# Query projections moved from the MLP blocks to the heads of the layers, and stored in the slots of their transposed input

## The chip, the cores and the metric

One Trainium2 chip, one of its cores. The time is the device time of one execution in microseconds (us). A kernel is run several times, alternating with the kernel before on the same chip; I quote medians with the lowest and highest run. Ratios are the mean time of one kernel's fast runs over the mean time of the other's fast runs of the same rounds, so they are not quite the ratio of the medians that stand beside them. All runs here were of the fast state.

The engines: PE multiplies matrices (PEld is its weight load, which runs beside it: 1082.6 us of PE and 837.1 us of PEld in a span of 1149.5 us), DVE is the vector engine, ACT the scalar engine, POOL is GpSimd, SP starts transfers. The order of each engine's instructions is fixed by the program. In one run below PE idles for 2.09 us in front of a product that waits for DVE, and the ten projection matmuls that are next in its order start only behind it. A wait for a PSUM bank holds PE in the same way: 0.73 us, twice, in the second head of the changed kernel, and the twenty projection matmuls next in its order start behind it.

## The reference, cut to what matters

Two identical layers over 2048 tokens of width 576. Each has a linear attention with 32 heads of 18 channels, whose feature map is a softmax of the projection and one of its negative, and then a gated MLP of width 4608. The weights `w_phi` are folded into the query and key weights at the start of the kernel.

```python
phi_q = concat([softmax(pq), softmax(-pq)])     # pq = x @ Wq @ w_phi, per head of 18
phi_k = concat([softmax(pk), softmax(-pk)])
kv  = einsum("bhsf,bhsd->bhfd", phi_k, v)       # needs every token
num = einsum("bhqf,bhfd->bhqd", phi_q, kv)
o   = num / den                                 # then @ wo, and added to x
...
x = x + A(layernorm(x)); x = x + B(layernorm(x))    # B: (x@Wg * x@Wu) @ Wd
x = x + A(layernorm(x)); x = x + B(layernorm(x))
```

## The kernel before

The 2048 tokens are 16 tiles of 128. A layer begins with a head: keys and values are projected, and the key-value sum is formed, which must be complete before any token's numerator. After it come eight blocks of the MLP, of two tiles each. Within a block PE first does the gate and up matmuls in two halves of its rows at once, then the down matmuls. Queries and the output projection of the tiles of the next block are woven into the gate and up stage, their numerators (products with the key-value sum, which lies in `BD`) into the down matmuls. The keys and values of layer 2 are woven into the blocks of layer 1, up to the last two tiles, which can only be done after its last block: that is the second head.

A query projection inside a block runs in row halves too (18 matmuls of 64 rows), outside it in full height (10 matmuls of 128 rows). Its softmax starts from PSUM, and the two banks are held until DVE has subtracted the minimum:

```python
def softmax_front(self, st_, pz, Wm, km, crit, ev=None, rowonly=False):
    ...
    gots = yield ("acqn", ["pb"], 2, True)              # two PSUM banks
    yield from s.proj(st_, Wm, km, banks)               # PE
    # ACT copies both halves to psb in SBUF; DVE: maximum from psb,
    # two minima from PSUM; POOL subtracts the maximum
    ...
    for h in range(2):
        ops.append(Op(370, (lambda e, ...: e.tensor_tensor(d2h, pv, mnbh, ALU.subtract)), ...))   # DVE, from PSUM
    yield ("ops", "dve", ops)
    for bank in banks:
        yield ("rel", "pb", bank)
    # two exponentials on ACT, their sums on DVE, reciprocals on ACT, two multiplies on POOL
```

A static scheduler, part of the program that builds the kernel, decides the order of each engine's instructions and which of the free PSUM banks each takes. The layer input, normalized and transposed, lies in `xT`, laid out `[128, 5, 2048]`; it is read by the projections and then by gate and up.

## Time and profile before

| | before |
|---|---|
| time, median of 3 | 1154.15 us (1151.78 to 1157.53) |
| span of the profiled run, granted clock | 1149.5 us, 0.983 |
| PE busy | 1082.6 us, 94% |
| DVE, ACT, POOL busy | 54%, 33%, 24% |
| first gate/up of layer 1 | 121.1 us |
| blocks of layer 1, start to start (1 to 5) | 65.3 to 66.0 us |
| block 7 of layer 1 with the second head | 96.5 us |
| blocks of layer 2 (1 to 5) | 59.8 us |

The stages are read from the first gate/up matmul of each block. The page's slices of 1/40 of the span show where PE is not full: the first five slices, and the 23rd and 24th; in the 23rd the clock is lower too. Digits are tenths.

```profile
PE   5776899999999999999999589999999999999998
...
PEclk9899999999999999999999799999999999999999
```

One more view matters later. It is the timeline of PE and DVE around one stall inside a block of layer 2; the columns are start, duration, engine, line, instruction, and in brackets the idle time before it and what ended it.

```profile
884.64 1.35 DVE L968 TENSOR_REDUCE ss<-dd 128x64 f32<-128x1152 bf16 x1 [1.32 <-ACT dd L963]
...
885.91 1.28 DVE L1283 TENSOR_TENSOR hT<-ps,hT 128x512 bf16<-128x512 f32 x2
...
886.65 0.28 PE L1235 MATMUL ps<-xT,Wu 64*128 64x256 bf16 x1 [0.38 <-DVE hT L1283]
```

DVE is far from full, but the sum of a query softmax (1.35 us) stands in its queue ahead of the multiplies of the MLP that empty PE's banks, and PE stands idle for 0.38 us. (From start to start it loses more: the gate/up matmul before this one began at 886.00, and pairs begin 0.11 us apart otherwise, so 0.54 us are lost.)

### The profile page before, as it was taken

Reading aid. Unit: us, or ns where it says so; the run is one execution under the profiler, and the core shown is the slowest. Engines: PE = TensorE matmul, PEld = TensorE weight load, DVE = VectorE, ACT = ScalarE, POOL = GpSimd, SP = SyncE. Lnnn points to the kernel's source line nnn. Section 1 sums busy time; section 2 is a strip of 40 time slices with the busy share of each in tenths; the row PEclk is TensorE's granted clock in tenths of the full one; section 3 lists DMA queues with packets and bytes.
Section 4 is the critical chain, followed back from the end, with each engine's and each line's share of the span. In section 5 each row is a group of like instructions: output and inputs, shape, how many; then the busy total and the mean of one; then the engine's idle time right before and its main releaser. Section 6 shows DMA issues by size and latency. Waiting matters only on the chain.

```text
span 1149.5 us, 34128 instructions
## 1 busy us (share of the span) xinstructions
PE 1082.6 (94%) x15480; PEld 837.1 (73%) x15480; DVE 618.8 (54%) x1289; ACT 376.9 (33%) x860; POOL 281.1 (24%) x304
## 2 busy tenths in 40 slices
PE   5776899999999999999999589999999999999998
PEld 3555777869687786869687368686868686868685
DVE  7788665747465573746352666362636262624131
ACT  7675331504143250514231233140414041312120
POOL 5775230413133240403220222130303030200000
PEclk9899999999999999999999799999999999999999
DMA  8383137282533627271523211827171626353514
GB/s 184 85 297 141 28 79 171 35 208 35 166 67 96 138 34 198 35 197 27 156 64 117 70 22 26 228 34 208 35 200 37 187 50 175 68 149 83 156 43 135
DMA packets 181035, 128.25 MB, mean 112 GB/s; under 512 B 99354, under 2 KB 179738, under 8 KB 179738
## 3 DMA queue, kind: packets, MB, share of 16 engines
q1 hardware_dynamic: 180890, 126.07, 42.7%
q8 instruction: 121, 1.98, 0.7%
q14 instruction: 24, 0.20, 0.1%
HBM read 100.73 MB, written 2.36 MB: 90 GB/s over the span
## 4 chain that ended last, share of the span: by engine, by line
PE 83%; DVE 9%; ACT 4%; DMA 3%; POOL 1%; issue 1%; SPq 0%; DVEq 0%; ACTq 0%
PE ps L1235 44%; PE ps L1305 20%; PE ps L901 9%; PE ps L1308 3%; PE ps L889 2%; PE ps L1134 2%; DVE ss L968 2%; DMA wdr<-in_B_w_down_dram 2%; PE ps L1020 1%; DVE x_sb L1182 1%; POOL dd L979 1%; DVE mxmn L928 1%; DVE mxmn L933 1%; DVE hT L1283 1%; DVE dd L947 1%
## 5 line engine op out<-in xcount | busy, mean ns | idle before, releaser
L1235 PE MATMUL ps<-xT,Wu 64*128 64x256 bf16 x4608 | 589.6, 270 | 2.3 <-DVE hT L1283 1.9
L1235 PE MATMUL ps<-xT,Wg 64*128 64x256 bf16 x4608 | 588.2, 270 | 1.6 <-ACT xT L870 1.6
L1235 PEld LDWEIGHTS ps<-xT,Wu 64*128 64x128 bf16 x4608 | 432.0, 94 | 25.1 <-DVE hT L1283 5.3
L1235 PEld LDWEIGHTS ps<-xT,Wg 64*128 64x128 bf16 x4608 | 427.1, 94 | 29.1 <-issue 3.3
L1281 ACT CAST hT<-ps 128x512 bf16<-128x512 f32 x288 | 167.8, 583 | 558.9 <-PE ps L1235 519.6
L1283 DVE TENSOR_TENSOR hT<-ps,hT 128x512 bf16<-128x512 f32 x288 | 197.5, 689 | 200.7 <-ACT hT L1281 200.3
L1305 PE MATMUL ps<-wdr,hT 128*128 128x512 bf16 x960 | 247.2, 380 | 1.5 <-DMA wdr<-in_B_w_down_dram 1.3
L1235 PE MATMUL ps<-xT,Wr 64*128 64x256 bf16 x1152 | 199.0, 270 | 0.0
L1308 PE MATMUL ps<-wdr,hT 128*128 128x64 bf16 x960 | 185.0, 193 | 0.0
L979 POOL TENSOR_TENSOR dd<-dd,ss 128x576 bf16<-128x576 bf16 x124 | 143.7, 1180 | 148.7 <-ACT ss L975 144.9
L1305 PEld LDWEIGHTS ps<-wdr,hT 128*128 128x128 bf16 x960 | 93.8, 98 | 112.2 <-DMA wdr<-in_B_w_down_dram 4.5
L859 POOL TENSOR_SCALAR xln<-x_sb,nmean,rstd 128x576 bf16<-128x576 bf16 x104 | 62.6, 607 | 413.8 <-ACT rstd L848 358.7
L1330 DVE TENSOR_TENSOR x_sb<-ps,x_sb 128x512 bf16<-128x512 f32 x32 | 22.0, 686 | 205.1 <-PE ps L1308 205.1
L938 POOL TENSOR_TENSOR dd<-psb,mxmn 128x576 bf16<-128x576 bf16 x63 | 73.3, 1164 | 209.1 <-DVE mxmn L928 209.0
L968 DVE TENSOR_REDUCE ss<-dd 128x64 f32<-128x1152 bf16 x64 | 86.3, 1348 | 32.0 <-ACT dd L963 31.4
L1308 PEld LDWEIGHTS ps<-wdr,hT 128*128 128x128 bf16 x960 | 94.1, 98 | 0.0
L1235 PEld LDWEIGHTS ps<-xT,Wr 64*128 64x128 bf16 x1152 | 89.5, 94 | 5.2
L961 ACT ACTIVATE dd<-dd 128x576 bf16<-128x576 bf16 x64 | 43.6, 683 | 54.7 <-DVE dd L947 54.7
L925 ACT CAST psb<-ps 128x288 bf16<-128x288 f32 x128 | 47.4, 400 | 37.5 <-PE ps L901 20.5
L928 DVE TENSOR_REDUCE mxmn<-psb 128x32 f32<-128x576 bf16 x64 | 47.5, 743 | 21.7 <-ACT psb L925 21.4
L1305 PE MATMUL ps<-wdx,hT 128*128 128x512 bf16 x192 | 53.5, 380 | 0.0
L933 DVE TENSOR_REDUCE mxmn<-ps 128x16 f32<-128x288 f32 x128 | 52.0, 448 | 0.0
(87 smaller groups left out, 937.5 us busy)
## 6 DMA issues: line engine op xcount, KB each, us to landing
wdr<-in_B_w_down_dram SPq DMA_DIRECT2D x240, 288.0 KB, 3.8
wdx<-in_B_w_down_dram SPq DMA_DIRECT2D x48, 288.0 KB, 3.7
Wg<-in_B_w_gate_dram SPq DMA_DIRECT2D x4, 1152.0 KB, 12.5
Wu<-in_B_w_up_dram SPq DMA_DIRECT2D x4, 1152.0 KB, 15.2
x_sb<-in_A_x_dram SPq DMA_DIRECT2D x8, 288.0 KB, 3.2
out_dram<-x_sb SPq DMA_DIRECT2D x16, 144.0 KB, 2.4
Wraw<-in_A_wqkv_dram SPq DMA_DIRECT2D x8, 144.0 KB, 3.4
xT<-xln SPq DMA_TRANSPOSE x58, 2.6
```

The lines of the kernel that those rows point to most:

```text
L859: em = [(lambda e, j=j, a=a, b=b, c=c: e.tensor_scalar(xln[:, sl[j], a:b], x_sb[:, ss[j], c:c + b - a], s.nmean[:, sl[j]:sl[j] + 1], rstd[ ...
L901: out.append(Op(61, (lambda e, h=h, k=k, st=(i == 0 and k == 0), sp=(i == 1 and k == 3): e.matmul(s.ps[:, banks[h], 0:N], L[r, k, :], Wm[r ...
L928: ops = [Op(665, (lambda e: e.tensor_reduce(mxmn[:, pz, 0, :], p3, AX.X, ALU.max)), reads=[("psb", pz, 0), ("psb", pz, 1)], writes=[("mx", ...
L933: ops.append(Op(370, (lambda e, h=h, pv=pv: e.tensor_reduce(mxmn[:, pz, 1, 16 * h:16 * h + 16], pv, AX.X, ALU.min)), reads=[("pbd", bank)] ...
L938: yield ("alt", [(eng, [Op(dur, (lambda e: e.tensor_tensor(d1, p3, mxb, ALU.subtract)), reads=[("psb", pz, 0), ("psb", pz, 1), ("mx", pz)] ...
L968: Op(1320, (lambda e: e.tensor_reduce(ss[:, sm, :].rearrange("p (b g) -> p b g", b=2), e4, AX.X, ALU.add)), reads=s.ddk(sm, 0) + s.ddk(sm, ...
L979: yield ("alt", [(eng, [Op(dur, (lambda e, ev=ev, rb=rb: e.tensor_tensor(ev, ev, rb, ALU.mult)), reads=s.ddk(sm, br) + [("ss", sm)], write ...
L1235: out.append(Op(54.3, (lambda e, bank=bank, cs=cs, lhsT=lhsT, rhs=rhs, st=st, sp=sp: e.matmul(ps[:, bank, cs], lhsT, rhs, start=st, stop=s ...
L1281: yield ("ops", "act", [Op(540, (lambda e, gb=gb, p=p: e.copy(hT[:, p, :], ps[:, gb, :])), reads=[("gu", gb)], writes=[("hT", p)] + (s.raw ...
L1283: yield ("ops", "dve", [Op(625, (lambda e, ub=ub, p=p: e.tensor_tensor(hT[:, p, :], ps[:, ub, :], hT[:, p, :], ALU.mult)), reads=[("gu", u ...
L1305: ops.append(Op(d_pe(512), (lambda e, lhsT=lhsT, bank=bank, slot=slot, fi=fi, f=f: e.matmul(ps[:, bank, 0:512], lhsT, s.wslot(slot)[:, fi, ...
L1308: ops.append(Op(d_pe(64) + 3, (lambda e, lhsT=lhsT, sl=sl, slot=slot, fi=fi, f=f: e.matmul(ps[:, Z, 64 * sl:64 * sl + 64], lhsT, s.wslot(s ...
```

## The change

The intent: PE is idle for a third of the heads and hardly at all in the blocks. The change therefore projects fourteen of sixteen query tiles of each layer in the heads, in full height, and parks the result (576 channels) in the slot of the `xT` tile it came from, which is 640 wide; nothing else needs that tile's input any more. The softmax is done later from SBUF, so that it holds no PSUM bank; minimum and maximum are two reductions on DVE, and both subtractions go to POOL. For the slot to be contiguous the layout of `xT` becomes `[128, 16, 5, 128]`, and gate and up read two runs of 128 columns in place of one of 256.

```diff
-        self.xT = A("xT", [128, 5, S], BF16)
+        self.xT = A("xT", [128, NS, 5, 128], BF16)
...
+    def t_qproj(self, L, st_):
+        yield ("wait", ("w", "q"))
+        yield ("wait", ("kp", L, st_))          # key and value of the tile are done
+        yield ("wait", ("v", L, st_))
+        if L == 1:
+            yield ("wait", ("ain", 1, min(NS - 1, s.pqg + st_ // s.pqd)))
+        ...
+        yield from s.proj(st_, s.Wq, "Wq", banks)
+        for h in range(2):                      # ACT: PSUM -> the tile's slot in xT
+            yield ("ops", "act", [... e.copy(s.pq(st_)[:, 288 * h:288 * h + 288], s.ps[:, bank, 0:288]) ...])
+            yield ("rel", "pb", bank)
+
+    def stored_front(self, L, st_):
+        yield ("wait", ("pq", L, st_))
+        for br, alu in ((0, ALU.max), (1, ALU.min)):
+            yield ("ops", "dve", [... e.tensor_reduce(s.mxq[:, mq, br, :], p3, AX.X, alu) ...])
+        for br in range(2):
+            yield ("ops", "pool", [... e.tensor_tensor(d, p3, mb, ALU.subtract) ...])
+        yield from s.softmax_tail(sm, 0)
...
-            ps_ = yield ("acq", "psb")
-            sm = yield from s.softmax_front(st_, ps_, s.Wq, "Wq", ...)
+            if st_ >= 2: sm = yield from s.stored_front(L, st_)
...
-                    seq = [(W[r, k, fs], s.xT[r, k, tok]) for k in range(4)]
+                    seq = [(W[r, k, fs], s.xT[r, tok, k, :]) for k in range(4)]
...
+    def t_qps(self):
+        yield ("wait", ("dn", 1, NB - 1))
+        for st_ in range(2, NS):
+            yield ("go", s.t_qproj(2, st_), s.pqp[1] + (NS - st_) / 100.0, ...)
```

More of the change, by code (lines that the diff above doesn't have):

```diff
@@ L546, in __init__ @@
         self.urgent = 4
+        self.pqp = (5, 5)
+        self.pqg = 12
+        self.pqd = 100
+        self.pqn = (16, 16)
         self.qcrit = False
@@ L600, in alloc @@
         self.dd = A("dd", [128, self.NSM, 2, D], BF16)
+        self.mxq = A("mxq", [128, 2, 2, H], F32)
         self.ss = A("ss", [128, self.NSM, 2 * H], F32)
@@ L613, in alloc @@
         sc.pool("vx", self.NVX)
+        sc.pool("mq", 2)
         sc.pool("et", self.NET)
@@ L863, in t_ln @@
         for j in js:
-            tok = slice(128 * ss[j], 128 * ss[j] + 128)
             if fast:
@@ L869, in t_ln @@
                                         reads=[("xln", sl[j]), ("ident",)], writes=[("pbd", bank)], excl=[("pb", bank)]) for k in range(5)])
-                yield ("ops", "act", [Op(d_act(640, True), (lambda e, P=P, tok=tok: e.copy(xT[:, :, tok], P[:, 0:640].rearrange("p (k n) -> p k n", k=5))),
+                yield ("ops", "act", [Op(d_act(640, True), (lambda e, P=P, j=j: e.copy(xT[:, ss[j], :, :], P[:, 0:640].rearrange("p (k n) -> p k n", k=5))),
                                          reads=[("pbd", bank)], writes=[("xT", ss[j])], excl=[("pb", bank)])])
@@ L873, in t_ln @@
             else:
-                yield ("dma", s.g_xt[sl[j]], (lambda e, j=j, tok=tok: e.dma_start_transpose(xT[:, :, tok], xln[:, sl[j], :])),
+                yield ("dma", s.g_xt[sl[j]], (lambda e, j=j: e.dma_start_transpose(xT[:, ss[j], :, :], xln[:, sl[j], :])),
                        [("xln", sl[j])], [("xT", ss[j])], 128 * 640 * 2, False, True, 1250.0)
@@ L884, in proj @@
         s = self
-        tok = slice(128 * st_, 128 * st_ + 128)
-        L = s.xT[:, :, tok] if src is None else src
+        L = s.xT[:, st_, :, :] if src is None else src
         rd = (keys or [("xT", st_)]) + [(km,), (km, 0)]
@@ L912, in proj, with softmax_front @@
         yield ("boost", 0.0)
-    def softmax_front(self, st_, pz, Wm, km, crit, ev=None, rowonly=False):
+    def softmax_front(self, st_, pz, Wm, km, crit, ev=None, rowonly=False, pev=None):
         s = self
@@ L922, in softmax_front @@
         yield from s.proj(st_, Wm, km, banks)
+        yield ("sig", pev)
         for h in range(2):
@@ L958, in softmax_front, with pq, softmax_tail @@
         yield ("sig", ev)
+        yield from s.softmax_tail(sm, crit, pz)
+        return sm
+    def pq(self, st_):
+        return self.xT[:, st_, :, :].rearrange("p k n -> p (k n)")[:, 0:D]
+    def t_qproj(self, L, st_):
+        s = self
+        yield ("wait", ("w", "q"))
[3 more added lines that the diff above has]
+            yield ("wait", ("ain", 1, min(NS - 1, s.pqg + st_ // s.pqd)))
+        if st_ >= s.pqn[L - 1]:
+            yield ("when", lambda: s.sc.open)
+        gots = yield ("acqn", ["pb"], 2, True)
+        banks = [g_[1] for g_ in gots]
+        yield from s.proj(st_, s.Wq, "Wq", banks)
+        for h in range(2):
+            bank = banks[h]
+            yield ("ops", "act", [Op(d_actc(288), (lambda e, h=h, bank=bank: e.copy(s.pq(st_)[:, 288 * h:288 * h + 288], s.ps[:, bank, 0:288])),
+                                     reads=[("pbd", bank)], writes=[("xT", st_)], excl=[("pb", bank)])])
+            yield ("rel", "pb", bank)
+        yield ("sig", ("pq", L, st_))
+    def stored_front(self, L, st_):
+        s = self
+        yield ("wait", ("pq", L, st_))
+        sm = yield ("acq", "sm")
+        mq = yield ("acq", "mq")
+        p3 = s.pq(st_).rearrange("p (g e) -> p g e", e=DH)
+        for br, alu in ((0, ALU.max), (1, ALU.min)):
+            yield ("ops", "dve", [Op(720, (lambda e, br=br, alu=alu: e.tensor_reduce(s.mxq[:, mq, br, :], p3, AX.X, alu)), reads=[("xT", st_)], writes=[("mq", mq, br)])])
+        for br in range(2):
+            d = s.dd[:, sm, br, :].rearrange("p (g e) -> p g e", e=DH)
+            mb = s.mxq[:, mq, br, :].unsqueeze(2).to_broadcast([128, H, DH])
+            yield ("ops", "pool", [Op(1150, (lambda e, d=d, mb=mb: e.tensor_tensor(d, p3, mb, ALU.subtract)), reads=[("xT", st_), ("mq", mq, br)], writes=s.ddk(sm, br))])
+        yield ("rel", "mq", mq)
+        yield from s.softmax_tail(sm, 0)
+        return sm
+    def softmax_tail(self, sm, crit, pz=None):
+        s = self
+        dd, ss = s.dd, s.ss
         de1 = dd[:, sm, 0, :]
@@ L964, in softmax_front @@
                                  reads=[("dd", sm, 0)], writes=[("dd", sm, 0)])])
-        yield ("rel", "psb", pz)
+        if pz is not None:
+            yield ("rel", "psb", pz)
         e4 = dd[:, sm, :, :].rearrange("p b (g e) -> p b g e", e=DH)
@@ L981, in softmax_front @@
                            for eng, dur in (("pool", 1150), ("dve", 675))[:1 + (crit > 1)]])
-        return sm
     def t_v(self, L, st_):
@@ L1030, in t_ain @@
         yield ("go", s.t_v(L, st_), (11 if L == 2 and st_ >= NS - 2 else 6) + (NS - st_) / 100.0, "v%d_%d" % (L, st_))
-        sm = yield from s.softmax_front(st_, ps_, s.Wk, "Wk", 2 if st_ >= NS - 2 else 1 if L == 1 else 0, None, L == 2 and st_ < NS - 2)
+        sm = yield from s.softmax_front(st_, ps_, s.Wk, "Wk", 2 if st_ >= NS - 2 else 1 if L == 1 else 0, None, L == 2 and st_ < NS - 2, ("kp", L, st_))
         yield ("wait", ("v", L, st_))
@@ L1094, in t_aout @@
         yield ("wait", ("ld", "wo"))
-        ps_ = yield ("acq", "psb")
-        sm = yield from s.softmax_front(st_, ps_, s.Wq, "Wq", 2 if L == 1 and st_ < 2 and s.qcrit else 0, ("qp", L, st_), st_ >= s.urgent)
+        if st_ >= 2:
+            sm = yield from s.stored_front(L, st_)
+        else:
+            ps_ = yield ("acq", "psb")
+            sm = yield from s.softmax_front(st_, ps_, s.Wq, "Wq", 2 if L == 1 and st_ < 2 and s.qcrit else 0, ("qp", L, st_))
         yield ("sig", ("qf", L, st_))
@@ L1216, in gu_quad @@
         ps = s.ps
-        tok = slice(256 * b, 256 * b + 256)
+        tok = slice(2 * b, 2 * b + 2)
         rd = [("xT", 2 * b), ("xT", 2 * b + 1)]
@@ L1228, in part @@
                     cs = slice(256 * jj, 256 * jj + 256)
-                    seq = [(W[r, k, fs], s.xT[r, k, tok]) for k in range(4)]
+                    seq = [(W[r, k, fs], s.xT[r, tok, k, :]) for k in range(4)]
                     if tail:
-                        seq.append((s.Wr[r, fs], s.xT[r, 4, tok]))
+                        seq.append((s.Wr[r, fs], s.xT[r, tok, 4, :]))
                     for n, (lhsT, rhs) in enumerate(seq):
@@ L1235, in part @@
                         out.append(Op(54.3, (lambda e, bank=bank, cs=cs, lhsT=lhsT, rhs=rhs, st=st, sp=sp: e.matmul(
-                            ps[:, bank, cs], lhsT, rhs, start=st, stop=sp, skip_group_check=True)),
+                            ps[:, bank, cs].rearrange("p (a n) -> p a n", a=2), lhsT, rhs, start=st, stop=sp, skip_group_check=True)),
                             reads=rd + [(wk,), ("Wr",)], writes=[("gu", bank), ("row", bank, half)], excl=[("pb", bank)], mode=1,
@@ L1381, in t_q @@
                 yield ("wait", ("x1", L, 2 * b - 1))
+    def t_qps(self):
+        s = self
+        yield ("wait", ("dn", 1, NB - 1))
+        for st_ in range(2, NS):
+            yield ("go", s.t_qproj(2, st_), s.pqp[1] + (NS - st_) / 100.0, "pq2_%d" % st_)
     def t_layer1(self):
@@ L1395, in t_layer1 @@
         yield ("go", lns(), 7, "lns")
+        for st_ in range(2, NS):
+            yield ("go", s.t_qproj(1, st_), s.pqp[0] + (NS - st_) / 100.0, "pq1_%d" % st_)
         for b in range(NB):
@@ L1482, in l2 @@
             yield ("go", s.t_barrier(2), 9, "bar2")
+            yield ("go", s.t_qps(), 9, "qps")
             yield ("wait", ("x1", 1, NS - 1))
```

## The prediction

> **What bounds the kernel now.** I read the windows of the trace first, cut at the stages: the head of each layer (projections, softmaxes and the key-value sum, up to the first gate/up matmul) and the eight blocks of the gated MLP (gate/up, then down) that follow it. Columns: stretch, its length, busy time of PE, PEld, DVE, ACT and POOL with instruction counts, granted clock, DMA share, GB/s.
>
> ```profile
> 0.00:121.10 121.10, 81.59 (x702) 59.46 (x704) 100.36 (x223) 82.01 (x216) 74.06 (x84) 0.93 0.58 168
> ...
> 185.00:250.50 65.50, 65.35 (x986) 51.28 (x982) 38.08 (x80) 21.80 (x50) 18.51 (x20) 1.00 0.48 107
> ...
> 640.50:673.40 32.90, 19.48 (x151) 13.81 (x153) 24.48 (x58) 12.09 (x28) 6.77 (x6) 0.81 0.00 1
> 673.40:737.00 63.60, 62.93 (x912) 47.28 (x912) 35.29 (x76) 18.89 (x40) 15.55 (x16) 0.97 0.40 101
> ...
> 856.70:916.50 59.80, 59.34 (x891) 46.33 (x892) 27.58 (x58) 15.34 (x32) 9.26 (x10) 1.00 0.45 118
> ...
> 1036.10:1092.00 55.90, 55.82 (x831) 43.99 (x832) 17.50 (x34) 10.93 (x20) 2.41 (x4) 1.00 0.43 114
> ```
>
> In the blocks PE is busy for all but 0.1 to 0.5 us, and beside it and its weight loads no engine passes 60%: a block costs what its matmuls cost. In the heads PE is idle for 39.5 of 121.1 us and 13.4 of 32.9 us, DVE is the busiest engine, and the clock falls to 0.81 in the second. The blocks number sixteen and the heads two, so PE work moved from a block to a gap in a head is worth its whole PE time, provided it does not push the head.
>
> Then I asked what one query projection costs in a block. The groups by shape:
>
> ```profile
> L901 PE MATMUL ps<-Wq,xT 64*128 64x288 bf16 x468 | 44.0, 283 | 0.5 <-DVE x_sb L1182 0.3
> L889 PE MATMUL ps<-Wq,xT 128*128 128x288 bf16 x60 | 8.7, 295 | 0.0
> ```
>
> So 26 of the 32 are in row halves (18 matmuls each) inside blocks, and 6 in full height (10 each) in the heads. The timeline of one row-halved projection:
>
> ```profile
> 869.15 0.28 PE L901 MATMUL ps<-Wq,xT 64*128 64x288 bf16 x1
> 869.27 0.77 PE L901 MATMUL ps<-Wq,xT 64*128 64x288 bf16 x9
> ...
> 870.64 0.28 PE L901 MATMUL ps<-Wq,xT 64*128 64x288 bf16 x1
> 870.76 0.65 PE L901 MATMUL ps<-Wq,xT 64*128 64x288 bf16 x7
> ```
>
> Gate/up goes on at 869.77 and 871.13, so the two pieces take 0.62 + 0.49 = 1.11 us. A second price comes from two blocks: 59.8 us (with two query projections and two numerator products) minus 55.9 us (with neither) is 3.9 us; a numerator takes 0.62 us (839.75 to 840.37), which leaves 2.66 us for two, 1.33 each, including a wait of 0.4 us for DVE. I take 1.2.
>
> The second head, from its timeline:
>
> ```profile
> 640.60 2.58 PE L889 MATMUL ps<-Wk,xT 128*128 128x288 bf16 x10 [0.79 <-ACT xT L870]
> ...
> 646.90 1.40 PE L889 MATMUL ps<-Wk,xT 128*128 128x288 bf16 x10 [0.78 <-ACT xT L870]
> ...
> 657.04 2.08 PE L1020 MATMUL ps<-vx,dd 128*128 128x152 bf16 x17 [3.33 <-POOL dd L979]
> ```
>
> Ten full-height matmuls take 2.58 us when PE has been idle and 1.40 us otherwise (1.24 start to start in a run); PE waits over 3 us at a time for POOL and DVE.
>
> [...] 2.58 against 1.40 us, and gate/up pairs 0.21 us apart at 121.1 us against 0.109 us after 123.8. [...] POOL's multiply takes 1.73 us (655.25) beside a DVE multiply, 1.16 us alone. The new DVE work is reductions, so I add nothing for contention.
>
> **The change, part by part.** The instruction order of the changed kernel, built but not run, has 28 full-height and 4 row-halved query projections: 10 more full ones in the first head, 12 in the second. It leaves two row-halved in the first block of layer 1 (as before) and the two of layer 2's first tiles in layer 1.
>
> 1. *Removed from blocks.* Five blocks of layer 1 and six of layer 2 lose two each: 22 x 1.2 = 26.4 us, all on PE's path. Blocks of 65.5 become about 63.2, blocks of 59.8 about 57.4.
>
> 2. *Added in the first head.* 10 x 1.24 = 12.4 us of PE. The order puts two around the last value projections, four more before the last key-value sum, two more before the numerators (where two stood before), two between the last two transposes of the normalized input and two after them. Before, the last key-value sums started at 101.63, 103.26 and 106.33, each when its POOL multiply or value copy was ready. With the inserted work in PE's fixed order I count 102.1, 104.0 and 108.35: 2.0 us late at the barrier. The last transpose then comes at 121.9, and two projections (2.5 us) stand between it and gate/up, of which the 0.7 us copy of the transpose covers some: gate/up starts near 124.8, 3.7 us late. But PE has then been busy for 5 us, so the cold start of 121.1 to 123.7 (2.55 us at half rate, 1.25 lost) should vanish. Net cost 2.5 us.
>
> 3. *Added in the second head.* 12 x 1.24 = 14.9 us into a stretch (635.8 to 673.4) where PE is idle for about 17. Four projections come before the first key projection, which starts 1.6 us later but warm: 1.3 instead of 2.58, so its result is within 0.2 us. The first softmax then gains about 0.7, the second key projection comes 1.1 late behind two more, and after its softmax the key-value sum stands at +0.65. It is warm (1.2 instead of 2.08 us), two projections then delay the first numerator by 0.5, and the last one hides in the 2.4 us wait for the second normalization. Gate/up starts about 0.6 late; of the cold start (clock 0.97 over 63.6 us, 1.9 us lost) I count half as regained. Net -0.4 us.
>
> 4. *Beside other work.* A query softmax has on DVE 743 + 2 x 448 + 2 x 446 = 2531 ns before and 2 x 743 = 1486 ns after; POOL gets one more subtraction of 1164 ns. Per block DVE falls by 2.1 us and POOL rises from 9.3 to 11.6 of 57 us: neither bounds. The two evictions of 400 ns on ACT stay, in the head instead. The input's new layout makes gate/up read two runs of 128 columns instead of one of 256; each run is contiguous, and I count zero.
>
> Sum: -26.4 + 2.5 - 0.4 = -24.3 us, so 1154.15 - 24 = 1130 us.
>
> **The rivals.**
> *The heads take back the gain.* PE works in order; a projection waiting for a PSUM bank stops everything behind it, and ACT must empty two banks for each (12 x 0.8 = 9.6 us in the second head, where ACT was busy 12 of 33). In the first head the key-value sums hold three of eight banks. For it: DVE waits and bank waits stand on most of the inserted instructions. Against it: most copies fall where ACT was idle. If each head loses 5 us more, 1140.
> *The wide read slows.* Gate/up is 10,368 matmuls in pairs 109 ns apart; two nanoseconds a pair for the broken run would cost 10 us: 1140. Nothing in the trace shows it, as no matmul before reads a broken run.
> *A new wait in the blocks.* The softmax of a stored tile has one more serial POOL step, and the transposes share SP's queue with the down weights. If the blocks get back 1 us each, 1141. Against it: the softmaxes now start at the head of a block, long before their numerators.
> *More gain.* If the dearer price of 1.33 us holds and both cold starts vanish, -29 + 2 - 1 = -28: 1126.
>
> **Range and chances.** The removed work is certain to about 3 us either way, the heads to about 4, and the rivals all point upward, so 1122 to 1141. The 2% line is 1154.15 x 0.98 = 1131.1, nearly at my number: 0.50 for faster, 0.47 for the same, 0.03 for slower.
>
> **What would show it.** Right: blocks of 57.4 and 63.2 us, gate/up pairs still 109 ns apart, first gate/up near 125 us, the second head no longer than 38.5 us from the last down matmul to gate/up and its clock above 0.9. Wrong: a block period falling by less than 2 us with PE waits for POOL, DMA or ACT in it (step 1); gate/up later than 127 us (step 2); the second head over 41 us or still cold (step 3); pairs over 110 ns (step 4).

## The result

| | before | after |
|---|---|---|
| time, median | 1154.21 us | 1126.19 us (1124.66 to 1128.48, 4 runs) |
| ratio of the fast runs | | 0.976, 95% interval 0.973 to 0.979 |
| span of the profiled run, clock | 1149.5 us, 0.983 | 1122.8 us, 0.992 |
| PE busy, matmuls | 1082.6 us, 15480 | 1074.6 us, 15304 |
| DVE, POOL busy | 618.8, 281.1 us | 594.6, 314.1 us |

The kernel is faster by 2.4%. The outputs are correct. The page of the kernel after has these slices:

```profile
PE   5788999999999999999999889999999999999998
...
PEclk9899999999999999999999999999999999999999
```

PE's dip in the second head is nearly filled, and the clock no longer falls there (1.00 in its window, 0.81 before). The windows, cut at the same stages as in the prediction (stretch, length, busy PE, PEld, DVE, ACT, POOL with counts, clock, DMA share, GB/s):

```profile
0.00:124.10 124.10, 91.64 (x802) 68.20 (x802) 101.80 (x224) 88.25 (x234) 75.63 (x85) 0.94 0.58 164
...
248.70:311.40 62.70, 62.70 (x946) 48.47 (x944) 36.39 (x74) 19.73 (x46) 20.83 (x22) 1.00 0.48 111
...
622.60:662.40 39.80, 31.66 (x282) 23.22 (x281) 29.28 (x68) 21.42 (x56) 9.94 (x8) 1.00 0.09 30
662.40:723.50 61.10, 60.58 (x876) 45.97 (x876) 30.67 (x63) 16.35 (x35) 18.22 (x18) 0.97 0.41 105
...
837.60:894.70 57.10, 57.02 (x856) 45.25 (x856) 25.94 (x52) 14.05 (x28) 11.50 (x12) 1.00 0.46 122
...
1008.80:1064.80 56.00, 55.89 (x831) 43.91 (x832) 17.50 (x34) 10.94 (x20) 2.40 (x4) 1.00 0.43 114
```

A block of layer 2 has 856 matmuls in place of 891 and lasts 57.1 us in place of 59.8, without an idle microsecond. The stretch without queries in it (the last line) is what it was. The second head, from the last down matmul to gate/up, has 276 PE instructions in place of 156 (the window above takes in six matmuls of its neighbours) and is longer, 39.40 us in place of 37.51. The groups by shape:

```profile
L1289 PE MATMUL ps<-xT,Wu 64*128 64x256 bf16 x4608 | 583.0, 269 | 0.2 <-DVE hT L1337 0.2
...
L893 PE MATMUL ps<-Wq,xT 128*128 128x288 bf16 x280 | 37.5, 286 | 0.7 <-DVE dd L952 0.7
...
L905 PE MATMUL ps<-Wq,xT 64*128 64x288 bf16 x72 | 6.3, 283 | 0.0
```

280 full-height and 72 row-halved matmuls are 28 and 4 projections, as the order had said. The columns after the bar are total busy time, mean ns of one, and the idle time before the group. The same row of gate and up in the kernel before reads

```profile
L1235 PE MATMUL ps<-xT,Wu 64*128 64x256 bf16 x4608 | 589.6, 270 | 2.3 <-DVE hT L1283 1.9
```

so a matmul on two runs of columns takes 269 ns where one on a single run took 270. (The profile models the ends of matmuls. Their starts say the same: at full clock the pairs of gate and up begin 109 ns apart in both kernels.) The 1.9 us of waits for DVE are down to 0.2.

**Where the 26.6 us of the two profiles come from** (from the starts of the first gate/up matmul of each block, and the last down matmul of all):

| part | before | after | difference |
|---|---|---|---|
| up to the first gate/up | 121.10 | 124.14 | +3.04 |
| layer 1, block 0 | 63.11 | 60.55 | -2.56 |
| layer 1, blocks 1 to 5, sum | 328.23 | 314.97 | -13.26 |
| layer 1, block 6 | 64.43 | 64.35 | -0.08 |
| layer 1, block 7 with the second head | 96.49 | 98.37 | +1.88 |
| layer 2, block 0 | 63.68 | 61.16 | -2.52 |
| layer 2, blocks 1 to 5, sum | 299.00 | 285.22 | -13.78 |
| layer 2, block 6, and block 7 to its last down matmul | 109.11 | 109.76 | +0.65 |

The eleven blocks that lost their projections (layer 1, 1 to 5, and layer 2, 0 to 5) give back 29.56 us, or 1.34 us for each of 22 projections. Everything else together takes back 2.9 us.

### The profile page after: what moved, and what is told of

Read it like the earlier page. It is cut to its first block, busy times and chain, and to the rows that moved or that the text cites. A ratio compares the mean times of both kernels' runs of the same rounds, so it can differ in the third digit from the quotient of the medians.

```text
span 1122.8 us, 33731 instructions
## 1 busy us (share of the span) xinstructions
PE 1074.6 (96%) x15304; PEld 832.2 (74%) x15304; DVE 594.6 (53%) x1204; ACT 373.6 (33%) x860; POOL 314.1 (28%) x333
## 4 chain that ended last, share of the span: by engine, by line
PE 86%; DVE 6%; DMA 3%; ACT 2%; POOL 2%; issue 1%; SPq 0%; DVEq 0%; ACTq 0%
PE ps L1289 49%; PE ps L1359 21%; PE ps L905 6%; PE ps L893 3%; PE ps L1362 3%; PE ps L1188 2%; POOL dd L1031 2%; PE ps L1071 1%; DMA wdr<-in_B_w_down_dram 1%; DVE ss L1020 1%; DVE x_sb L1236 1%; DMA oT<-dd 1%; DVE st L839 1%; DMA wdx<-in_B_w_down_dram 0%; DVE mxmn L933 0%
## 5 line engine op out<-in xcount | busy, mean ns | idle before, releaser
L1289 PE MATMUL ps<-xT,Wu 64*128 64x256 bf16 x4608 | 583.0, 269 | 0.2 <-DVE hT L1337 0.2
L1289 PE MATMUL ps<-xT,Wg 64*128 64x256 bf16 x4608 | 581.8, 269 | 0.8 <-ACT xT L875 0.8
L1289 PE MATMUL ps<-xT,Wr 64*128 64x256 bf16 x1152 | 188.4, 270 | 0.0
L1002 POOL TENSOR_TENSOR dd<-xT,mxq 128x576 bf16<-128x576 bf16 x56 | 63.8, 1163 | 312.8 <-DVE mxq L998 312.8
L1289 PEld LDWEIGHTS ps<-xT,Wr 64*128 64x128 bf16 x1152 | 81.2, 94 | 5.6
L943 POOL TENSOR_TENSOR dd<-psb,mxmn 128x576 bf16<-128x576 bf16 x35 | 40.7, 1164 | 82.7 <-DVE mxmn L933 82.6
L839 DVE BATCH_NORM_STATS2 st<-x_sb 128x6 f32<-128x288 bf16 x128 | 49.3, 446 | 3.0 <-DMA x_sb<-in_A_x_dram 2.8
L905 PE MATMUL ps<-Wo,oT 64*128 64x288 bf16 x504 | 43.5, 283 | 1.7 <-DMA oT<-dd 0.8
## 6 DMA issues: line engine op xcount, KB each, us to landing
Wg<-in_B_w_gate_dram SPq DMA_DIRECT2D x4, 1152.0 KB, 12.2
```

The source lines that it names most:

```text
L839: ops.append(Op(d_dve(288), (lambda e, j=j, h=h: e.bn_stats(st[:, sl[j], 6 * h:6 * h + 6], x_sb[:, ss[j], 288 * h:288 * h + 288])), reads= ...
L905: out.append(Op(61, (lambda e, h=h, k=k, st=(i == 0 and k == 0), sp=(i == 1 and k == 3): e.matmul(s.ps[:, banks[h], 0:N], L[r, k, :], Wm[r ...
L1002: yield ("ops", "pool", [Op(1150, (lambda e, d=d, mb=mb: e.tensor_tensor(d, p3, mb, ALU.subtract)), reads=[("xT", st_), ("mq", mq, br)], w ...
L1289: out.append(Op(54.3, (lambda e, bank=bank, cs=cs, lhsT=lhsT, rhs=rhs, st=st, sp=sp: e.matmul(ps[:, bank, cs].rearrange("p (a n) -> p a n" ...
```

## The experiments

Twelve runs, in four calls, two of them of the changed kernel itself; "before" in each call is the kernel before, run in the same rounds. Its median was 1154.4, 1155.2, 1154.2 and 1155.0 us.

### The form alone

Is it the stored form (fewer DVE instructions, banks freed sooner) or the place of the projection? Here the projections stay row-halved in their blocks, but go through `xT` and the new softmax.

```diff
-        for st_ in range(2, NS):
-            yield ("go", s.t_qproj(1, st_), ...)
...
-            yield ("go", s.t_qps(), 9, "qps")
...
+                if st_ >= s.urgent:
+                    yield ("when", s.in_row)     # inside the block's row-halved stretch
...
+                yield from s.t_qproj(L, st_)
```

> The changed kernel, but each query projection stays in the block where it was before, row-halved; only the stored form of its softmax is kept (minimum and maximum taken from the stored copy, both subtractions on POOL). Theory A (the gain is PE work taken out of the blocks, 1.11 us a projection, plus a short wait for DVE that goes with the lighter query softmax): layer-2 blocks of 57.05 + 2 x 1.11 = 59.3 us with no PE wait for DVE left, whole kernel near 1154 - 11 x 0.5 = 1148 us. Rival B (the lighter softmax on DVE is what paid, not the place of the projection): blocks near 57 us, below 1140 us. If the wait belongs to the projection and not to the softmax's form: blocks of 59.8 us, 1154 us.

Measured: 1152.92 us, ratio 0.999 (0.998 to 1.001). One window of a layer 2 block, cut like the earlier ones:

```profile
801.31:860.61 59.30, 59.22 (x891) 46.90 (x890) 25.96 (x52) 15.23 (x32) 11.61 (x12) 1.00 0.45 119
```

The number of matmuls is that of before (891), the idle time is 0.08 us, and the block is 59.3 us in place of 59.8. PE's waits for DVE in front of the up matmuls fell to 0.2 us in all. So the form is worth 0.5 us a block in layer 2. In layer 1 it is worth nothing: blocks of 65.27 to 65.6 us. That is part of why the time came out 5 us above the 1148 that I had expected. From 59.3 to the 57.05 us of the changed kernel there remain 2.25 us, or 1.13 for a projection: that is the place.

In layer 1 the place is worth 2.70 us a block (65.27 against 62.57), and the starts of PE's instructions say where the other 0.45 us are. An output projection is one of the places. Here it waits for DVE; in the changed kernel's block (the second line) it does not:

```profile
328.68 1.15 PE L905 MATMUL ps<-Wo,oT 64*128 64x288 bf16 x10
```

```profile
324.31 0.78 PE L905 MATMUL ps<-Wo,oT 64*128 64x288 bf16 x10
```

The ten matmuls of the first take longer because one of them starts 0.36 us after the one before it, where 0.12 is usual. In the same block a value projection starts 0.1 us late, and a gate/up pair 0.07 us later than in the changed kernel. The weight loads in front of the first two name DVE: over the kernel they sit idle for it for 3.7 us at the output projections (2.6 in the changed kernel) and for 0.9 us at the value projections (none there). For the pair I take it to be the same wait, as an estimate. All three come again in each of the three blocks of 65.27 us, and in the changed kernel's blocks of 62.57 us the first two are gone. Most of this doesn't show as idle time (0.15 us a block), since the modelled end of a matmul lies some 0.3 us behind its start and hides a shorter wait.

### The layout alone

The kernel before with the other layout of `xT` and nothing else.

```diff
-        self.xT = A("xT", [128, 5, S], BF16)
+        self.xT = A("xT", [128, NS, 5, 128], BF16)
...
-                    seq = [(W[r, k, fs], s.xT[r, k, tok]) for k in range(4)]
+                    seq = [(W[r, k, fs], s.xT[r, tok, k, :]) for k in range(4)]
```

> The kernel before with the new layout of the transposed input alone (tile by tile, gate/up reading two runs of 128). Theory A: nothing, 1154 us within 2 us, gate/up pairs 109 ns apart, blocks of 59.8 us. Rival C (the layout speeds the transposes or the matmuls and is part of the gain): 1150 us or less, and a shorter gate/up stage in the block that has no query projection (38.05 us before).

Measured: 1154.06 us, ratio 1.000 (0.999 to 1.002); blocks of layer 2 at 59.8 us, as before. The broken read costs nothing that can be seen.

### One projection's price inside a block

The changed kernel with the output projection of twelve tiles of layer 2 done twice, in row halves, in blocks 0 to 5.

```diff
+        if L == 2 and 2 <= st_ < 14:
+            banks = banks[::-1]
+            yield from s.proj(st_, s.Wo, "Wo", banks, s.oT[:, oTb, :, :], [("oT", oTb)])
```

> The changed kernel with the output projection of the layer-2 tiles 2 to 13 done twice, the second into the same two banks swapped, in row halves: 18 more matmuls a tile and nothing else, no eviction, no softmax. It prices PE work alone. Theory A: 1.11 us each, blocks of 57.05 + 2.22 = 59.3 us, whole kernel 1126 + 13.3 = 1139.5 us. If the 1.37 us that a query projection gave back is all PE time: blocks of 59.8 us, 1142.5 us.

Measured: 1139.81 us, ratio 0.987 (0.984 to 0.990). One block:

```profile
783.95:843.10 59.15, 59.15 (x891) 46.70 (x890) 25.77 (x51) 14.03 (x28) 11.54 (x12) 1.00 0.46 117
```

891 matmuls again, no idle time, 59.15 us. The two projections cost 2.11 us in the gate and up stage (40.80 in place of 38.69), 1.05 each. (From start to start the 18 matmuls of one take 1.10 us; 0.1 us of an old wait for DVE went.) So 1.05 to 1.13 us is the price in PE time alone of a row-halved projection in layer 2, from two sides, and the 0.5 us of DVE waits is what makes 2.75 us of two.

### The heads alone

The kernel before with 22 projections more, in full height in its heads, whose results are thrown away; the projections in the blocks stay.

```diff
+            yield ("ops", "act", [... e.copy(s.scr[:, :], s.ps[:, bank, 0:288]) ...])   # nobody reads scr
...
+        for st_ in range(4, 14):
+            yield ("go", s.t_extra(1, st_), ...)
...
+        for st_ in range(4, NS):
+            yield ("go", self.t_extra(2, st_), ...)
```

> The kernel before with 22 more full-height query projections in the two heads, evicted to a scratch tile and thrown away; the blocks keep their own. It prices the heads alone. Theory A (they fall mostly into idle PE time, as in the changed kernel: gate/up of layer 1 three us later but warm, the second head 1.9 us longer): 1154 + 2 to 4, so 1156 to 1158 us. If the heads pay for them in full: 22 x 1.24 = 27, so 1181 us. If warming PE is worth more than the delay: 1153 or less.

Measured: 1157.11 us, ratio 1.002 (1.000 to 1.003). Some 27 us of PE work (22 x 1.24) cost 2.7 us. The second head is as long as before (block 7 with it 96.58 us against 96.49), and the block behind it was 62.17 us in place of 63.68. So twelve projections do fit into the second head for nothing, and the 1.9 us that the changed kernel pays there must come from something else.

### Layer 1 alone

The changed kernel with layer 2 as in the first experiment.

```diff
-            yield ("go", s.t_qps(), 9, "qps")
...
+            if L in (2,):
+                yield from s.t_qproj(L, st_)     # in the block, row-halved
```

> The queries of layer 1 are projected in its head and stored, as in the changed kernel; those of layer 2 stay row-halved in its blocks, but in the stored form of the first experiment. Theory (each projection taken out of a block gives back its 1.1 us, in either layer, and the heads cost little): layer 1's blocks as in the changed kernel (62.6), layer 2's blocks 1 to 5 as in the first experiment (59.3), and the second head about 37.5 us from the last down matmul; twelve projections at 1.1 us dearer than the changed kernel, less some 2 us of a shorter second head: 1126.2 + 13.2 - 2 = about 1137. Rival (the gain came from layer 1 alone, or mainly from the clock of the second head): under 1131, or the whole of it lost, over 1150.

Measured: 1141.04 us (1136.73 to 1144.54), ratio 0.988 (0.986 to 0.991), 4 us more than expected. The steady blocks came out as expected: layer 2's at 59.3 us, layer 1's at 62.6. The difference is in block 0 of layer 2, which I had left out: it too holds two projections again and took 65.56 us against 61.16, some 2.1 us more than 2.25 for the two; what made these was not shown. With it, 5 x 2.25 + 4.4 - 1.0 for the shorter head is 14.7 us. The measured difference is 14.8 from the 1126.2 of the result, but 12.2 from the changed kernel of the same rounds (1128.85, below), and 13.4 between the two profiles. So the gain is additive over the layers to within some 2 us; the rival, a gain that sits in one layer or in the clock, is out.

### Half of the projections of layer 2 back in a block

Tiles 8 to 15 of layer 2 are projected inside block 0, in row halves, into the same slots.

```diff
-        self.pqn = (16, 16)
+        self.pqn = (16, 8)      # from this tile on: only inside a block
```

> The changed kernel, but of layer 2's twelve moved projections only those of tiles 2 to 7 are in the head; the eight of tiles 8 to 15 run row-halved inside block 0 of layer 2, into the same stored form. Theory (an inside projection costs 1.1 us of PE, the head's own cost is a wait of up to 2 us that goes with fewer projections): block 0 is 8 x 1.1 = 8.8 us longer, the second head up to 2 us shorter, so 7 to 9 us dearer than the changed kernel: 1133 to 1135. Rival (the projections aren't hidden in the head but only cheaper there, at 1.37 us each of PE time): the head is 8 x 1.37 = 11 us shorter and the time no more than the changed kernel's, 1126 or less.

Measured: 1134.92 us (1132.52 to 1137.64), ratio 0.983 (0.981 to 0.986). The block and the middle of the head:

```profile
664.47:734.21 69.74, 69.74 (x1020) 55.29 (x1021) 31.94 (x64) 23.18 (x52) 19.76 (x20) 0.96 0.39 92
```

```profile
640.00:656.00 16.00, 7.79 (x58) 6.03 (x59) 9.51 (x21) 2.94 (x7) 2.69 (x2) 0.57 0.00 0
```

The block is 8.6 us longer than in the changed kernel's first profile (1.07 for each projection; the clock in it is 0.96 and 0.97), as expected. The head did the opposite of what I expected: with eight projections fewer it is longer, 99.99 us with block 7 in place of 98.37. PE is busy for 7.8 of 16 us there, and its clock is 0.57. In the changed kernel the same head, from the last down matmul to gate/up, has clock 1.00, here 0.73: the clock was up with the filling and fell without it.

### The changed kernel again, and what a single profile is worth

No edit: two more runs of the same kernel.

> The changed kernel itself again, so that the three others can be compared with it on the same chip: 1126.2 within 1 us, ratio to the kernel before 0.9757 within 0.002. If it comes out elsewhere, differences under that size between the others are not read.

> The changed kernel on the same chip and in the same rounds as the two beside it. 1126 to 1129, ratio 0.9757 to 0.9774 as in its two earlier looks; its profile shows how much the first head alone varies from one execution to the next (first gate and up at 124.1 and 130.0 so far).

Measured: 1128.85 us, ratio 0.977 (0.975 to 0.980), and 1125.88 us, ratio 0.976 (0.973 to 0.978). The first gate/up came at 129.98 and 124.06 us in these two profiles and at 124.14 in the first: the same instructions, 6 us apart. In two experiments whose first head has PE's order of before it came at 123.79 (the layout) and 125.32 (the form), against 121.10. So the +3.04 us of the table above cannot be read as the cost of the change as it stands. It can be read from a mark inside the head: a key-value sum that stands in front of the first inserted projection. In the kernel before, in the changed kernel's first profile and in its second it is

```profile
96.52 0.78 PE L1020 MATMUL ps<-vx,dd 128*128 128x152 bf16 x10 [1.63 <-POOL dd L979]
```

```profile
95.92 0.78 PE L1071 MATMUL ps<-vx,dd 128*128 128x152 bf16 x10 [1.63 <-POOL dd L1031]
```

```profile
100.09 0.80 PE L1071 MATMUL ps<-vx,dd 128*128 128x152 bf16 x10 [1.51 <-POOL dd L1031]
```

So 4.2 of the 6 us lie before anything that the change touched; the other 1.7 lie behind the mark (29.89 us from there to gate/up in the second profile). From the mark to gate/up it is 24.58 us in the kernel before and 28.22 in the first and the third profile of the changed kernel: 3.64 us later. In the two other executions with the order of before it is 26.05 us (the form) and 26.41 (the layout), with PE at half rate for part of it: ten query matmuls of the form took 2.59 us, where 1.39 is usual, and five value matmuls of the layout 1.40, where 0.78 is. In the kernel before, too, five value matmuls took 1.41 us there. Against the two the change costs 1.8 to 2.2 us.

The second head is steadier, 98.37, 98.36 and 99.07 us with block 7, and 39.40, 39.38 and 39.38 from the last down matmul to gate/up. Block 0 of layer 2 was 61.16 us at clock 0.97, then 60.21 and 59.49 at 1.00.

### The second head: three orders of the same work

Where do 1.9 us go, when twelve thrown-away projections cost nothing? The timeline of PE of the changed kernel, from the key-value sum to the first numerator, the matmuls that read `BD`:

```profile
643.41 0.36 PE L1071 MATMUL ps<-vx,dd 128*128 128x152 bf16 x3
644.45 0.37 PE L1071 MATMUL ps<-vx,dd 128*128 128x152 bf16 x3 [0.68 <-POOL dd L1031]
645.55 0.58 PE L1071 MATMUL ps<-vx,dd 128*128 128x152 bf16 x8 [0.73 <-DVE kvacc L1112]
646.86 0.57 PE L1071 MATMUL ps<-vx,dd 128*128 128x152 bf16 x6 [0.73 <-DVE kvacc L1112]
647.27 2.61 PE L893 MATMUL ps<-Wq,xT 128*128 128x288 bf16 x20
649.72 0.78 PE L1188 MATMUL ps<-BD,eT 128*128 128x152 bf16 x12
```

Two things stand out. The sum comes in three pieces with a wait for DVE's addition between them: all three parts were given the same PSUM bank, since the scheduler saw the others taken by projections that wait for ACT. And after it two projections (2.6 us) stand in front of the numerator. The first edit takes the three banks together:

```diff
+        if b == NB - 1:
+            gots = yield ("acqn", ["pb"], 3)
         for bi in range(3):
-            (_, bank), = yield ("acqn", ["pb"], 1)
+            bank = gots[bi][1]          # for the last block; one by one otherwise
```

> The changed kernel with one edit: the key-value sum of the last block of layer 1 asks for its three banks together, where it asked for one after another and got the same bank three times. Theory (the second head's 1.9 us more are the queue of query evictions in front of that sum): the sum takes some 2 us in place of 4.0, the second head 37.5 to 38 us in place of 39.4, and the time is 1.2 to 1.9 us less than the changed kernel's. Rival (the head is longer because PE is full with projections, 31.7 us of 39.8, or because VectorE is): the sum is shorter and gate and up begin no earlier; the time within 0.5 us of the changed kernel's.

Measured: 1123.93 us (1122.9 to 1125.37), ratio 0.974 (0.972 to 0.976). By the medians that is 4.9 us better than the changed kernel of the same call, but the profiles say that this is not the head: block 7 with it is 98.37 us, as before the edit, and the difference lies in the first head (124.5 against 130.0 us). The timeline:

```profile
644.71 1.17 PE L1071 MATMUL ps<-vx,dd 128*128 128x152 bf16 x17 [1.91 <-POOL dd L1031]
...
645.72 4.29 PE L893 MATMUL ps<-Wq,xT 128*128 128x288 bf16 x20
...
649.85 0.79 PE L1193 MATMUL ps<-BD,eT 128*128 128x152 bf16 x12
```

The sum is in one piece and ends 1.8 us earlier relative to POOL's last product, as my theory had it, and nothing is won: the two projections behind it ran at half rate for most of their time (4.29 us in place of 2.61), after PE had waited 1.91 us for POOL. The edit did more than I meant: with three banks held for the sum the scheduler put nine projections in front of it in place of ten, and so the wait grew from 0.68 to 1.91 us. That goes against my theory, and half against its rival. The next edit holds those two projections back too:

```diff
+        if L == 2 and st_ in (11, 12):
+            yield ("wait", ("num", 2, 0))        # after the first numerator in PE's order
+        if L == 2 and st_ >= 13:
+            yield ("wait", ("num", 2, 1))
```

A sister kernel has no projection there either, leaves the banks to the scheduler, and has ten projections in front of the sum where this one has nine:

```diff
+        if L == 2 and st_ in (12, 13):
+            yield ("wait", ("num", 2, 0))
+        if L == 2 and st_ >= 14:
+            yield ("wait", ("num", 2, 1))
```

> The key-value sum of the second head with its three banks at once, as in the run before, and besides no stored query projection between that sum and the first numerator in PE's order (two of twenty matmuls stood there, 2.6 to 4.3 us of PE); one of the later projections now stands behind the last transpose in front of gate and up. Theory (the second head is 1.9 us longer than before because that sum and then these two projections stand ahead of the first numerator in PE's order): the first numerator starts some 3.9 us after GpSimd's last product, as in the kernel before, in place of 5.2; gate and up come 1.3 us earlier, less up to 0.6 for the projection at the end: block 7 with the head 97.5 us in place of 98.4. Rival (the head is bound by VectorE or by the clock, which drops when PE idles there): the numerator is earlier and the head as long as before, 98.4 or more, or the clock of the head falls under 0.95.

> Only the order of the run beside it without its banks: no projection between the key-value sum and the first numerator, but the sum still takes its banks one after another behind the evictions of ten projections. Theory that the queue in front of the sum costs by itself: the sum takes 4 us as in the changed kernel, the first numerator starts 4.5 us or more after GpSimd's last product, the head is 0.7 to 1.3 us longer than that of the run beside it. Rival (the projections in front of the numerator were the whole cost, the sum's banks none): both heads alike within 0.3 us.

Measured: 1125.72 us, ratio 0.975 (0.973 to 0.977), and 1125.62 us, ratio 0.975 (0.973 to 0.977). The second of the two did not test what it was made for: with the other order its sum got three banks by itself and ran in one piece of 1.18 us. The first one's timeline:

```profile
643.50 1.18 PE L1075 MATMUL ps<-vx,dd 128*128 128x152 bf16 x17 [1.91 <-POOL dd L1035]
646.76 1.33 PE L1197 MATMUL ps<-BD,eT 128*128 128x152 bf16 x12 [2.09 <-DVE BD L1142]
647.89 2.60 PE L893 MATMUL ps<-Wq,xT 128*128 128x288 bf16 x10
650.29 1.35 PE L1197 MATMUL ps<-BD,eT 128*128 128x152 bf16 x12
```

The numerator does start early, 3.3 us after POOL's last product. But PE has idled for 1.91 and 2.09 us with 1.18 us of work between, and runs at half rate: the numerator takes 1.33 us in place of 0.78, the next ten matmuls 2.60 in place of 1.39. Block 7 with the head is 98.70 us, and 98.83 in its sister. The rival was right here. Not all of the loss is the clock: in both kernels one projection has moved behind the last transpose, and gate/up starts 1.6 us after that transpose in place of 1.2.

So the traces show two effects: with two projections there the numerator is later, and with none the clock fell (granted 0.50 from 646 to 650 us in the first of the two kernels), and from the numerator to gate/up it took 15.01 and 14.34 us in place of 12.66. How surely the clock falls is open, as each kernel but the changed one has a single profile. In the run with the doubled output projection, whose second head has the changed kernel's order and the same three gaps, the clock fell as well (granted 0.50 from 647 to 649 us), while three executions of the changed kernel stayed at full rate after gaps of 0.68, 0.73 and 0.73 us:

```profile
645.38 0.58 PE L1071 MATMUL ps<-vx,dd 128*128 128x152 bf16 x8 [0.73 <-DVE kvacc L1112]
646.69 0.94 PE L1071 MATMUL ps<-vx,dd 128*128 128x152 bf16 x6 [0.73 <-DVE kvacc L1112]
```

Its head took 40.82 us. How busy PE must be for its clock to stay up is not settled here. The last kernel puts exactly one there, by gates on the changed kernel alone:

```diff
+        if L == 2 and st_ in (13, 14):
+            yield ("wait", ("num", 2, 0))
+        if L == 2 and st_ >= 15:
+            yield ("wait", ("num", 2, 1))
```

> The changed kernel with the second head in the order that the run with thrown-away projections had, whose head was as long as that of the kernel before: four projections in front of the key-value sum, one (not two, not none) between the sum and the first numerator, one between the two numerators, the rest later. Theory (the head is longest where projections delay the numerator, and as long where none stands there, because PE then idles and its clock drops; one projection does neither): clock 0.98 or more in the head, the first numerator 3.3 to 3.9 us after GpSimd's last product, block 7 with the head 96.6 to 97.4 us in place of 98.4 to 99.1, and the time 1 to 2 us under the changed kernel's (ratio 0.974 to 0.975). Rival (the 2 us come with the stored form, whose minimum, maximum and evictions load VectorE and ScalarE, wherever the projections stand): 98.2 us or more.

Measured: 1124.54 us (1119.92 to 1126.59), ratio 0.973 (0.970 to 0.975).

```profile
649.48 1.18 PE L1075 MATMUL ps<-vx,dd 128*128 128x152 bf16 x17 [0.68 <-POOL dd L1035]
650.49 1.39 PE L893 MATMUL ps<-Wq,xT 128*128 128x288 bf16 x10
652.74 0.79 PE L1192 MATMUL ps<-BD,eT 128*128 128x152 bf16 x12 [0.86 <-DVE BD L1137]
```

The sum is in one piece (with this order it got three banks by itself), the numerator comes 3.3 us after POOL's last product, and it runs at full rate. Side by side, from the timelines (us):

| kernel | projections between sum and numerator | POOL's last product to first numerator | from there to gate/up | last down matmul to gate/up | block 7 with head |
|---|---|---|---|---|---|
| before | 1 (ten matmuls) | 3.95 | 12.43 | 37.51 | 96.49 |
| heads alone | 1 | 3.32 | 12.42 | 37.60 | 96.58 |
| after | 2, sum in pieces | 5.33 | 12.66 | 39.40 | 98.37 |
| after, three banks | 2, half rate | 5.19 | 12.81 | 39.40 | 98.37 |
| after, none between | 0 | 3.32 | 15.01 | 39.73 | 98.70 |
| its sister | 0 | 3.32 | 14.34 | 39.06 | 98.83 |
| after, one between | 1 | 3.32 | 12.43 | 37.15 | 96.65 |

The last row is the best version found. By its profile the head, from the last down matmul, is 2.2 us shorter than in each of the changed kernel's three profiles (37.15 against 39.38 to 39.40), though I have only one profile of it. By the times (ratio 0.973 against 0.976, 0.977 and 0.976) it is the fastest in ratio, but the intervals overlap, and a gain of 0.2% is no more than suggested by them.

## Why the prediction was right or wrong

The time, 1126.2 us, is inside the range and 3.8 us under the number. The main step held: PE work taken from blocks that PE bounds comes back whole, and put into the gaps of the heads it costs little. That the sum came so near is in part luck: by the table of parts the blocks gave 3.2 us more than forecast and the first head cost 2.0 us less, the second head cost 2.3 us more, and these errors partly cancel.

1. *Removed from blocks.* The mechanism was right and the term was sized too small: -29.56 us for 22 projections in place of -26.4, or 1.34 each in place of 1.2. Two prices lay on the table, 1.11 from the starts in the timeline and 1.33 from the difference of two blocks, and I took a middle. For layer 2 the parts are now measured. PE's own share is 1.05 (doubled output projection) to 1.13 (form alone against the changed kernel); the "wait of 0.4 us for DVE" is the other 0.5 us a block, and it went as well, since the softmax's DVE work is smaller and holds no bank. Being a wait of the very thing that was removed, it belonged in the price. Predicted blocks of 57.4 and 63.2 us came out at 57.05 and 62.6 to 64.0. In layer 1 the price is 1.35 though the form alone gives nothing there; the 0.2 us more a projection are waits for DVE too (0.25 us at an output projection, 0.1 at a value projection and, by my estimate above, 0.07 at gate/up in a block), which went with the projections and not with the form. So the 1.11 us from the timeline was right for PE's work, and both layers add waits to it.

2. *Added in the first head.* +2.5 us was predicted. Measured up to the start of block 1 it is +0.48: gate/up 3.04 later ("near 124.8" against 124.14), block 0 2.56 shorter, for which the heads alone show 1.2 (61.93 us with no other change to that block). Counted from the mark inside the head, the step held in this pair of profiles. The last key-value sum starts 9.81 us behind the mark before and 11.66 after, 1.85 us late at the barrier where 2.0 was forecast, and gate/up is 3.64 us late where 3.7 was. Block 0 gave back more than the 1.25 us forecast for a warm start: in the first 2.6 us of gate/up the clock was 0.50 before and 1.00 after. The sign that I had set, gate/up later than 127 us, was a bad one: the second profile shows 129.98 us, and most of that arose in front of the inserted work.

3. *Added in the second head.* This is the step that failed. Up to POOL's last product it held: the key projections started 1.3 and 1.2 us later (1.6 and 1.1 were forecast) and warm (1.39 us for the ten matmuls of the first, 2.58 before), and the product ended 0.3 us later (0.65 forecast). I had -0.4 us in all, with the sum "warm (1.2 instead of 2.08 us)" and a numerator delayed by 0.5. The last down matmul to gate/up took 39.4 us, over the 38.5 that I had set as its limit, though under the 41 that I had called wrong. The key projections were warm and the clock 1.00, as predicted, but the sum took 4.0 us in three pieces, and the numerator came 1.4 us late: 0.9 because the sum ended 3.04 us after POOL's last product (2.14 before), 0.5 for the two projections behind it. Of the 2.0 us by which the numerator comes earlier in the best version, 1.8 lie in the sum and 0.2 in the projections; no run separates the two cleanly, since each edit moved other projections too. The half of the cold start to be regained was not regained in the first profile (clock 0.97 in block 0 in both kernels) and was in the next two (1.00). I had read the order of PE's instructions and not which bank each would take, and the order alone doesn't show that. The best order shows the price: with one projection between and the sum in one piece, the head with block 7 is 96.65 us, as long as before.

4. *Beside other work.* In the window of a layer 2 block DVE fell from 27.58 to 25.94 us, 1.6 in place of the 2.1 predicted; POOL rose from 9.3 to 11.5, against 11.6 predicted. Neither bounds anything. For contention I had added nothing: the 56 new subtractions on POOL took 1.159 to 1.166 us each, the one at 649.51, beside a DVE reduction for part of it, too. The layout costs zero, by its own experiment and by 269 against 270 ns.

Of the rivals, "the heads take back the gain" is out for the first head's size and holds in small for the second, where the bank of the sum and the order cost 1.9 of the feared 5 us. "The wide read slows" is out, by the layout alone. "A new wait in the blocks" is out: 57.02 of 57.10 us are PE work. "More gain" at 1126 was the nearest, for its first reason, the dearer price; it points downward, so the prediction's sentence that its rivals all point upward was wrong.

## What to carry to other kernels

When an engine is full in one stage and waits on chains in another, move its work there and price it from the difference of two whole stages with and without it, not from its own instructions, since the waits it brings go with it (here 0.5 of the 2.75 us of two projections). In the stage that receives the work, what counts is what stands just in front of each instruction of the chain in the engine's fixed order, and which buffer the chain's instruction was given: some 2 us of 39 hung on where one projection stood, and on the bank that the sum was given. And filler can have a second use, for here PE's clock was up with it (1.00 in the second head, 0.73 with eight projections fewer): in the one profile of each, taking out the projections that stood in the way (98.70 and 98.83 us) was no better than leaving two (98.37). Where executions differ at the start, count from a mark in front of the change.
